# Attention without scaled probabilities: the inverse row sums go to the values' partitions and scale two heads' output at once

## The chip, the cores and the metric

The kernel runs on one core of a Trainium2 chip. The metric is the device time of one execution in microseconds (us). Three runs of the kernel before took 854.75, 860.95 and 860.27 us, median 860.27. One further execution was recorded by the profiler. The engines are TensorE (PE, with its weight loads as PEld), VectorE (DVE), ScalarE (ACT), GpSimd (POOL) and SyncE (SP, which issues nearly all transfers).

## The reference

```
scores = q @ k.T / 8                      # 4 batches, 8 heads, 576 tokens, head size 64
bias   = -(cum[q] - cum[k])               # cum = running sum of max(s, 0)
scores = where(causal, -1e9, scores + minimum(bias, 0))
attn   = exp(scores - max); attn = attn / (sum(attn) + 1e-9)
x      = attn @ v                         # heads side by side: 576 x 512 per batch
h      = relu(x @ w_in)                   # first mixer, 1024 wide
x      = (h * sigmoid(conv3(h))) @ w_out
u      = x + mix of tokens by U, V (rank 32)
out    = u + relu(u @ w_ch1) @ w_ch2      # second mixer, 2048 wide
```

All of it is float32; weights and small parameters arrive as 64-bit numbers and are decoded on the chip.

## The kernel before, in words

There are 32 heads, worked through one by one, and two heads (a *pair*) fill the 128 rows of one x tile. For a head, `scores` (L700) makes four score tiles of 128 query rows, 128 to 512 keys wide: TensorE multiplies (L690), VectorE adds the mask and takes the maximum in one pass (`top`, L651), ScalarE takes the exponential into an SBUF tile P and sums the rows on the way (`exps`, L668). The 64 query rows left over of both heads of a pair share a fifth tile (`scores4`, L730; in the profile's names `p`).

Once the fourth tile's sum is there, VectorE adds 1e-9 and inverts the four sums (L724, L725), and `normalise` (L676, L679) has GpSimd multiply P by them, row by row: four operations per head, 128 to 512 wide, and one of 576 per pair for `p`. Then `transp` (L785, L793) turns P by TensorE transposes in four groups; ScalarE (and for all but the first eight heads VectorE, which makes a low part) copies them to SBUF, and `av` (L809, L829) multiplies them with the values. The result is x transposed: its rows are the head size, two heads on top of each other, its columns are the tokens. When the second head of a pair is done, x is split into a high and a low part by ScalarE and GpSimd (L874, L875), and the first mixer (`m1_in` L893, `m1_out` L935) can use it. The mixer's matmuls for one batch run beside the next batch's attention. Behind attention come the last batch's first mixer, then the second mixer in two parts (L1174, then L1270).

P has two sets of buffers, so the exponentials of head h+2 have to wait for the transposes of head h. The q and k rows of each head are placed by SP transfers (`place`, L630) from tiles that GpSimd and VectorE split before (L618, L619).

The order of the instructions is not the order of the text. A planner (`Plan.order`, L183) lists every operation with its cost and its predecessors, and issues on each engine the earliest in the text that is ready by its own clock. Each engine, and SP's queue too, then works strictly in that order on the chip. PSUM has eight banks, given out by class (`CAPS`).

Of the kernel before, what the change touches and what calls it, by code (L numbers as in the profile page):

```python
# [8 lines left out]
F32 = mybir.dt.float32  # L9
# [35 lines left out]

RECIP = (3,)

CAPS = dict(sc=3, pt=1, av=5, h=4, y=4, tp=2, t1=4, mh=1, ma=8, my=8, mx=2)

RINGS = dict(P=2, qk=2, th=3, vv=2, qkh=1, x=2, wf=2, xs=5, g=12, hh=3, c=3, x2=4, w64=2, mh=5, o=4, snap=2, tt=4)  # L50

# [258 lines left out]
def tile_attention_moe_mixer(  # L310
# [60 lines left out]
    dram = ctx.enter_context(tc.tile_pool(name="dram", bufs=1, space=DRAM))  # L371
    r_t = dram.tile([NH, 4, 2, S], F32R, name="r_d")
    r_d = Buf(None, None, None, None, "r_d")
    u_t = [dram.tile([128, KT, S], F32, name=f"u_d{b}") for b in range(B)]
    u_d = [Buf(None, None, None, None, "u") for b in range(B)]
    ch_t = [dram.tile([128, NTOK], F32, name=f"ch_d{f}") for f in range(NF2)]
# [187 lines left out]


    xs = {}

    def p_tiles(g):
        return [ring(ap, f"P{i}_", RINGS["P"], [128, 128 * (i + 1)], F32, f"P{g}_{i}") for i in range(4)] + [
# [103 lines left out]
            186,  # L673
        )

    def normalise(t, w, r, key, keys):  # L676
        pool(
            w,
            lambda: nc.gpsimd.tensor_scalar(t[:, :w], t[:, :w], r(), 1.0, ALU.mult, ALU.mult),  # L679
            [key] + keys,  # L680
            keys,
            extra=208,
        )

    def products(h, ps, rows, q0, k0, w):
        d = st[h]

        def mms():
            for c, t in enumerate(d["qk"]):
                nc.tensor.matmul(  # L690
                    ps[:rows, :w],
                    lhsT=t[:, 0, q0 : q0 + rows],
                    rhs=t[:, 1, k0 : k0 + w],
                    start=c == 0,
                    stop=c == len(d["qk"]) - 1,
                )

        pe(16 + 1.88 * w if h in FS else 2 * mm(w, rows), mms, d["qk"], [ps])

    def scores(h, i):  # L700
        P, sm = st[h]["P"][i], st[h]["sm"]
# [14 lines left out]
        if i in RECIP:  # L716
            ns = range(max((x + 1 for x in RECIP if x < i), default=0), i + 1)
            ss = [(sm, f"s{n}") for n in ns]
            rs = [(sm, f"r{n}") for n in ns]

            def r():
                return sm[:, 8 + ns[0] : 9 + i]

            dve(2, lambda: nc.vector.tensor_scalar(r(), sm[:, 4 + ns[0] : 5 + i], 1e-9, None, ALU.add), ss, rs)  # L724
            dve(15, lambda: nc.vector.reciprocal(r(), r()), rs, rs)  # L725
            for n in ns:
                Pn = st[h]["P"][n]
                normalise(Pn, 128 * n + 128, lambda n=n: sm[:, 8 + n : 9 + n], (sm, f"r{n}"), [Pn])

    def scores4(h):  # L730

# [18 lines left out]
        for n, ps in enumerate(tiles):  # L750
            exps(
                lambda n=n: P[:, n * HS : n * HS + HS],
                ps,
                128,
                HS,
                lambda: sm[:, 1:2],
                lambda n=n: sm[:, 2 + n : 3 + n],
                (sm, "m1"),
                [(P, n), (sm, f"s{n}")],
            )  # L760
        dve(
            60,
            lambda: nc.vector.scalar_tensor_tensor(
                sm[:, 4:5], sm[:, 2:3], 1e-9, sm[:, 3:4], ALU.add, ALU.add
            ),
            [(sm, "s0"), (sm, "s1")],
            [(sm, "r")],
        )
        dve(15, lambda: nc.vector.reciprocal(sm[:, 4:5], sm[:, 4:5]), [(sm, "r")], [(sm, "r")])
        normalise(P, S, lambda: sm[:, 4:5], (sm, "r"), [(P, 0), (P, 1)])  # L770


    GROUPS = [[(0, 0, 1), (1, 1, 1)], [(0, 2, 4), (3, 3, 4)], [(1, 2, 4), (4, 4, 4)], [(2, 2, 4)]]
# [35 lines left out]
    def av(h, half):  # L809
# [53 lines left out]
        if hh % 2 == 1 and half == 1:  # L863
            th = ring(xp, "xh", RINGS["xs"], [128, S + 2], F32R, f"xh{b}_{dt}")
            tl = ring(xp, "xl", RINGS["xs"], [128, S + 2], F32R, f"xl{b}_{dt}")
            for t in (th, tl):
# [4 lines left out]
                    [],  # L871
                    [(t, "pad")],
                )
            hi_act(lambda: th[:, 1 : S + 1], x, [x], [(th, "x")], S)  # L874
            lo_pool(lambda: tl[:, 1 : S + 1], x, lambda: th[:, 1 : S + 1], [x, (th, "x")], [(tl, "x")], S)  # L875
            xs[b, dt] = (th, tl)
# [451 lines left out]
    def att_head(h):  # L1328
# [28 lines left out]
            transp(h - 1, 3)  # L1357
        if h < NH and h % 2 == 0:
            scores4(h)
        if h > 0:  # L1360
            av(h - 1, 1)

# [206 lines left out]
```

## Time and profile before

| what | value |
|---|---|
| runs | 854.75, 860.95, 860.27 us |
| profiled execution | 857.56 us, of which the span from first to last instruction 855.7 us |
| TensorE, weight loads | 95%, 86% of the span busy |
| VectorE, ScalarE, GpSimd | 71%, 54%, 43% |
| granted TensorE clock, mean | 0.995 |
| transfers | 123.31 MB, mean 144 GB/s |

The first matmul starts at 8.4 us. The share of an engine over the whole span hides the stages: attention by itself until about 100 us, attention with the first mixer until about 390, then the mixers. A wait is given to the one that came last of what an instruction waited for. A busy TensorE is not TensorE at its peak, since matmuls overlap and their ends are modelled; the weight loads' share shows more of the gaps.

### The profile page before, as it was taken

The numbers are of one execution on the slowest core, as the hardware profiler recorded it, in microseconds if no ns is written. First come the engines' busy times: TensorE is split into PE (matmuls) and PEld (weight loads), VectorE is DVE, ScalarE is ACT, GpSimd is POOL, SyncE is SP. The second block draws the span as 40 slices with busy tenths as digits, with TensorE's granted clock in tenths as the row PEclk, the third lists the DMA queues.
The fourth block names the chain that finished last, engine by engine and source line by source line (L and its number), as shares of the span: only waits on it lengthen the run. The fifth ranks groups of instructions, "written<-read, shape, count | busy, mean of one in ns | idle before, by whom it ended". The sixth has DMA issues, their size and how long they took to land. (4 is left out here: it accounts for less than half of the span.)

```text
span 855.7 us, 15636 instructions
## 1 busy us (share of the span) xinstructions
PE 813.2 (95%) x5300; PEld 738.0 (86%) x5300; DVE 610.0 (71%) x1362; ACT 459.9 (54%) x1144; POOL 365.3 (43%) x461
## 2 busy tenths in 40 slices
PE   5889899999999999999999989999999999999998
PEld 2556689889999998998999889999998888888888
DVE  6865899986997769978878998777878762323232
ACT  4776888875987668875766423223233432222211
POOL 4675777574455734457345663333344220000000
PEclk9998999999999999999999999999999999999999
DMA  6868844573455524512133336445467764545443
GB/s 198 234 161 199 202 136 121 141 188 80 122 131 146 129 58 128 149 51 82 34 115 121 118 107 204 145 144 179 138 188 235 256 203 121 163 123 165 130 123 99
DMA packets 67624, 123.31 MB, mean 144 GB/s; under 512 B 9412, under 2 KB 34884, under 8 KB 67544
## 3 DMA queue, kind: packets, MB, share of 16 engines
q1 hardware_dynamic: 67472, 122.30, 50.1%
q8 instruction: 42, 0.69, 0.3%
q14 instruction: 38, 0.31, 0.1%
q10 hardware_dynamic: 72, 0.01, 0.0%
HBM read 68.88 MB, written 28.90 MB: 114 GB/s over the span
## 5 line engine op out<-in xcount | busy, mean ns | idle before, releaser
L1270 PE MATMUL my<-mh,w 128*128 128x512 f32 (+1 forms) x560 | 158.9, 368 | 0.0
L1174 PE MATMUL ma_S<-u,W 128*128 128x288 f32 x768 | 119.2, 296 | 7.6 <-DVE s L1190 7.5
L1251 DVE SCALAR_TENSOR_TENSOR ml<-ml,mh 128x512 fp32r<-128x512 f32 (+1 forms) x80 | 51.9, 654 | 98.3 <-ACT mh L1248 98.3
L935 PE MATMUL y<-gh,w1o 128*128 128x288 f32 x512 | 118.1, 301 | 0.7 <-DVE c L914 0.4
L1270 PEld LDWEIGHTS my<-mh,w 128*128 128x128 f32 x560 | 101.6, 189 | 17.4
L1174 PEld LDWEIGHTS ma_S<-u,W 128*128 128x128 f32 x768 | 107.5, 188 | 10.2 <-DVE s L1190 10.0
L1248 ACT ACTIVATE mh<-ml 128x512 fp32r<-128x512 f32 (+1 forms) x80 | 46.9, 589 | 118.8 <-DMA ml<-ch_d 74.0
L679 POOL TENSOR_SCALAR P<-P,sm 128x128 f32<-128x128 f32 (+3 forms) x128 | 74.9, 602 | 82.2 <-DVE sm L725 61.4
L1270 PE MATMUL my<-ml,w 128*128 128x512 f32 (+1 forms) x280 | 103.0, 368 | 0.0
L1174 PE MATMUL ma_A<-u,W 128*128 128x288 f32 x576 | 92.9, 296 | 0.5 <-DVE s L1190 0.4
L935 PEld LDWEIGHTS y<-gh,w1o 128*128 128x128 f32 x512 | 86.4, 188 | 2.2 <-DVE c L914 1.1
L651 DVE CUSTOM_DVE_ANT_0 sc<-sc,mask 128x128 f32<-128x128 f32 (+2 forms) x144 | 68.8, 494 | 24.3 <-PE sc L690 17.1
L1174 PEld LDWEIGHTS ma_A<-u,W 128*128 128x128 f32 x576 | 81.8, 188 | 1.4 <-DVE s L1190 0.9
L365 POOL TENSOR_TENSOR gl<-c,gh 128x288 fp32r<-128x288 f32 x64 | 53.9, 846 | 64.3 <-ACT gh L920 60.7
L893 PE MATMUL h<-xh,w1h 128*128 128x290 f32 x256 | 80.0, 313 | 0.5 <-DVE c L914 0.5
L893 PE MATMUL h<-xl,w1h 128*128 128x290 f32 x256 | 76.4, 298 | 0.7 <-POOL xl L365 0.7
L893 PE MATMUL h<-xh,w1l 128*128 128x290 f32 x256 | 76.3, 298 | 0.0
L935 PE MATMUL y<-gl,w1o 128*128 128x288 f32 x256 | 75.1, 293 | 0.6 <-POOL gl L365 0.6
L668 ACT ACTIVATE P<-sc,sm 128x128 f32<-128x128 f32 (+3 forms) x128 | 67.5, 530 | 11.2 <-DVE sm L651 9.5
L905 DVE SCALAR_TENSOR_TENSOR c<-h,cw,c 128x288 f32<-128x288 f32 x128 | 64.3, 509 | 5.3 <-ACT c L901 4.3
L1186 ACT COPY p<-ma_A 128x288 f32<-128x288 f32 x64 | 25.5, 399 | 73.0 <-PE ma_A L1174 57.7
L362 DVE TENSOR_TENSOR tl<-pt,th 128x384 fp32r<-128x384 f32 x96 | 54.3, 566 | 12.4 <-ACT th L353 12.1
(145 smaller groups left out, 1990.6 us busy)
## 6 DMA issues: line engine op xcount, KB each, us to landing
ml<-ch_d SPq DMA_DIRECT2D x64, 256.0 KB, 2.6
ch_d<-s SPq DMA_DIRECT2D x64, 144.0 KB, 1.8
raw_w<-w_in SPq DMA_DIRECT2D x16, 512.0 KB
raw_w2a<-w_in SPq DMA_DIRECT2D x16, 512.0 KB, 4.7
raw_w2b<-w_in SPq DMA_DIRECT2D x16, 512.0 KB, 4.4
t<-qk_in SPq DMA_DIRECT2D x28, 288.0 KB, 2.9
qkA<-t SPq DMA_DIRECT2D x56, 144.0 KB, 4.0
qkA<-t SPq DMA_DIRECT2D x28, 288.0 KB, 3.0
```

Of the source, the lines that this page charges most:

```text
L362: dve(n, lambda: nc.vector.tensor_tensor(out(), src(), f32(hi()), ALU.subtract), r, w)
L365: pool(n, lambda: nc.gpsimd.tensor_tensor(out(), src(), f32(hi()), ALU.subtract), r, w, two=True)
L651: lambda: nc.vector.tensor_tensor_reduce(out=ps[:rows, :w], in0=ps[:rows, :w], in1=mask[:rows, m0 : m0 + w], scale=-0.125, scalar=3.0e38 i ...
L668: lambda: nc.scalar.activation(out(), ps[:rows, :w], ACTF.Exp, bias=low(), scale=-1.0, accum_out=total()),
L679: lambda: nc.gpsimd.tensor_scalar(t[:, :w], t[:, :w], r(), 1.0, ALU.mult, ALU.mult),
L893: nc.tensor.matmul(ps[:, :W], lhsT=ww, rhs=xx, start=kt + n == 0, stop=kt == KT - 1 and n == 2)
L905: lambda k=k: nc.vector.scalar_tensor_tensor(c(), hh[:, k : k + HS], cw[:, 3 * f + k : 3 * f + k + 1], c(), ALU.mult, ALU.add),
L935: nc.tensor.matmul(ps[:, :HS], lhsT=ww, rhs=xx(), start=f + n == 0, stop=f == NF1 - 1 and n == 2)
L1174: nc.tensor.matmul(ps[:, :HS], lhsT=ww, rhs=uu, start=k == 0, stop=k == 5)
L1248: act(n, lambda: nc.scalar.activation(mh[:, :n], raw(), ACTF.Relu), [ml], [mh])
L1251: lambda: nc.vector.scalar_tensor_tensor(ml[:, :n], raw(), 0.0, f32(mh[:, :n]), ALU.max, ALU.subtract),
L1270: nc.tensor.matmul(ys[c][dt][:, :n], lhsT=ww, rhs=xx[:, :n], start=f + k == 0, stop=f == NF2 - 1 and k == 2)
```

## The change

P stays as the exponential left it. The inverse sums of both heads of a pair go into one small tile `rr` of nine columns: four for each head and one for the shared tile. A new function `spread` transposes `rr` on TensorE to nine rows of 128 (a new PSUM class `rt`), ScalarE copies them to SBUF, SP writes them to DRAM (`rv_d`), and four more SP transfers read them back, each repeated over 64 partitions, into a tile R of 128 x 576: for each row of x the inverse sum of that token in that head. Before x is split, GpSimd multiplies x by R. The nine columns transposed hold the sums in the order of the tokens.

```diff
-    def normalise(t, w, r, key, keys):
-        pool(
-            w,
-            lambda: nc.gpsimd.tensor_scalar(t[:, :w], t[:, :w], r(), 1.0, ALU.mult, ALU.mult),
...
+    def inverse(h):
+
+        if h not in rrs:
+            rrs[h] = ring(ap, "rr", 2, [128, 9], F32, f"rr{h}")
+        return rrs[h]
...
-            for n in ns:
-                Pn = st[h]["P"][n]
-                normalise(Pn, 128 * n + 128, lambda n=n: sm[:, 8 + n : 9 + n], (sm, f"r{n}"), [Pn])
...
-        normalise(P, S, lambda: sm[:, 4:5], (sm, "r"), [(P, 0), (P, 1)])
+        dve(15, lambda: nc.vector.reciprocal(rr[:, 8:9], rr[:, 8:9]), [(rr, 8)], [(rr, 8)])
+
+    def spread(h):
+
+        rr = inverse(h)
+        ps = bank("rt", f"rt{h}")
+        pe(120, lambda: nc.tensor.transpose(ps[:9, 0:128], rr(), ident[:, 0:128]), [ident, rr], [ps])
+        rw = ring(ap, "rw", 1, [9, 128], F32, f"rw{h}")
+        act(128, lambda: nc.scalar.copy(rw(), ps[:9, 0:128]), [ps], [rw])
+        rv, d = rv_t[h // 2], Buf(None, None, None, None, f"rv{h}")
+        dma(4608, lambda: nc.sync.dma_start(out=rv, in_=rw()), [rw], [d])
+        R = ring(ap, "R", 1, [128, S], F32, f"R{h}")
+        for a in range(2):
+            half = slice(64 * a, 64 * a + 64)
+            dma(
+                131072,
+                lambda a=a, half=half: nc.sync.dma_start(
+                    out=R[half, 0:512],
+                    in_=rv[4 * a : 4 * a + 4].rearrange("a b -> (a b)").partition_broadcast(64),
+                ),
+                [d],
+                [(R, a)],
+            )
+            dma(
+                16384,
+                lambda half=half: nc.sync.dma_start(out=R[half, 512:S], in_=rv[8, half].partition_broadcast(64)),
+                [d],
+                [(R, 2 + a)],
+            )
+        return R
...
+            R = spreads.pop(h - 1)
+            pool(S, lambda: nc.gpsimd.tensor_tensor(x(), x(), R(), ALU.mult), [x, R], [x], two=True)
             hi_act(lambda: th[:, 1 : S + 1], x, [x], [(th, "x")], S)
...
+        if h < NH and h % 2 == 1:
+            spreads[h - 1] = spread(h - 1)
```

Since the planner decides, the order on every engine moves. Three places show it.

GpSimd at the third pair of the first batch, before: `P_0` to `P_3` and `p_1` are the scaling, `w1o` the low part of a weight, `t_8` the split of q and k, `xl_2` the split of the pair's x.

```order
L356 TENSOR_SCALAR t_8_738<-t_8_753 128x576
L679 TENSOR_SCALAR P_0_759<-P_0_759,sm_169 128x128
L679 TENSOR_SCALAR P_1_774<-P_1_774,sm_169 128x256
L679 TENSOR_SCALAR P_2_781<-P_2_781,sm_169 128x384
L679 TENSOR_SCALAR P_3_815<-P_3_815,sm_169 128x512
L365 TENSOR_TENSOR w1o<-wf_w_1_512_786,w1o 128x512
L679 TENSOR_SCALAR p_1_147<-p_1_147,sm_1_396 128x576
L365 TENSOR_TENSOR xl_2_117<-x_2_724,xh_2_115 128x576
L365 TENSOR_TENSOR w1o<-wf_w_2_512_847,w1o 128x512
```

The same place in the change, with the new product of x and R:

```order
L356 TENSOR_SCALAR t_8_759<-t_8_775 128x576
L365 TENSOR_TENSOR w1o<-wf_w_0_512_822,w1o 128x512
L901 TENSOR_TENSOR x_2_726<-x_2_726,R_794 128x576
L365 TENSOR_TENSOR xl_2_133<-x_2_726,xh_2_131 128x576
L365 TENSOR_TENSOR w1o<-wf_w_1_512_892,w1o 128x512
L365 TENSOR_TENSOR w1o<-wf_w_2_512_926,w1o 128x512
```

The five scalings are gone, one product stands before the split of x, and the weight parts have moved behind it.

TensorE at the first head, in the change: `pt` are its transposes of P, `tf` their copies, `sc` the third head's scores, `rt` the new transpose.

```order
L855 MATMUL av_1_294<-tf_2_296,vr_146 64x320
L683 MATMUL sc_0_313<-ws 128x128
L683 MATMUL sc_1_317<-ws 128x256
L855 MATMUL av_1_294<-tf_3_310,vr_146 64x320
L773 MATMUL rt_327<-ident,rr_220 9x128
L855 MATMUL av_1_294<-tf_1_270,vr_146 64x192
L855 MATMUL av_1_294<-tf_2_296,vr_146 64x64
L819 MATMUL pt_0_339<-ident,P_1_267 128x128 x2
```

Before, the two score tiles `sc_0` and `sc_1` stood ahead of the second group of `pt` of the first head; now they stand behind all of them, and the `rt` transpose lies between the last products with the values, with the next head's transposes behind it.

SP's queue at the second pair, in the change: `t_6` is the load of the next pair's q and k, `qkA` and `qkB` are their placement.

```order
L620 DMA t_6_469<-qk_in 128x576
L777 DMA rv_d_59<-rw_536 9x128
L783 DMA R_574<-rv_d_59 64x512
L792 DMA R_574<-rv_d_59 64x64
L783 DMA R_574<-rv_d_59 64x512
L792 DMA R_574<-rv_d_59 64x64
L640 DMA qkB_170<-r_d 4x1152
L640 DMA qkB_170<-t_6_428 64x1152
L640 DMA qkA_634<-t_6_469 64x1152
```

Here the four reads follow the write directly, and the placements of the next head stand behind; at most other pairs the loads of the next pair's q and k stand between write and reads.

## Rows read from the trace of the kernel before

**Rows 1.** The page's first part: busy us, share of the span, instructions.

```profile
PE 813.2 (95%) x5300; PEld 738.0 (86%) x5300; DVE 610.0 (71%) x1362; ACT 459.9 (54%) x1144; POOL 365.3 (43%) x461
```

**Rows 2.** Busy time by stretch: us, each engine, granted clock, DMA share, GB/s.

```profile
20.00:100.00 80.00, 69.45 (x372) 47.37 (x371) 57.20 (x153) 58.93 (x162) 53.84 (x62) 0.96 0.78 199
100.00:150.00 50.00, 47.20 (x343) 44.84 (x342) 48.22 (x131) 43.28 (x123) 38.19 (x51) 1.00 0.54 139
150.00:380.00 230.00, 225.09 (x1666) 215.35 (x1665) 186.97 (x517) 177.64 (x488) 123.48 (x200) 1.00 0.48 123
```

**Rows 3.** Waits from 20 to 100 us: total us, times, longest.

```profile
PEld pt L793 <- POOL p L679: 6.9, 5, 2.4
...
PE pt L793 <- POOL p L679: 3.4, 3, 2.0
...
PE av L829 <- DMA vr<-vP_in: 2.7, 2, 2.3
```

**Rows 4.** TensorE's waits from 100 to 380 us, the longest.

```profile
PE pt L793 <- ACT P L668: 2.0, 2, 1.0
```

**Rows 5.** Timeline around one wait: start, us, engine, what, idle before.

```profile
73.67 3.18 POOL L679 TENSOR_SCALAR P<-P,sm 128x128 f32<-128x128 f32 x4 [2.01 <-DVE sm L725]
...
74.47 0.49 ACT L668 ACTIVATE p<-sc,sm 128x288 f32<-128x288 f32 x1
...
76.81 1.69 POOL L365 TENSOR_TENSOR w1o<-wf_w,w1o 128x512 fp32r<-128x512 f32 x1
...
78.49 0.74 POOL L679 TENSOR_SCALAR p<-p,sm 128x576 f32<-128x576 f32 x1
...
79.28 0.18 PEld L793 LDWEIGHTS pt<-ident,p 128*128 128x128 f32 x1 [2.43 <-POOL p L679]
```

**Rows 6.** GpSimd's groups: busy us, mean ns, idle before them.

```profile
L679 POOL TENSOR_SCALAR P<-P,sm 128x128 f32<-128x128 f32 (+3 forms) x128 | 74.9, 602 | 82.2 <-DVE sm L725 61.4 <-ACT P L668 8.1 <-ACT raw_w2a L502 6.1
...
L365 POOL TENSOR_TENSOR xl<-x,xh 128x576 fp32r<-128x576 f32 x16 | 19.4, 1213 | 4.8 <-ACT xh L353 4.5
...
L679 POOL TENSOR_SCALAR p<-p,sm 128x576 f32<-128x576 f32 x16 | 13.3, 828 | 1.3 <-DVE sm L769 1.3
```

**Rows 7.** Busy time in three short stretches.

```profile
60.00:65.00 5.00, 3.55 (x10) 1.85 (x11) 2.08 (x3) 1.21 (x3) 3.98 (x4) 0.72 1.04 216
75.00:80.00 5.00, 3.00 (x17) 2.17 (x17) 3.56 (x12) 3.92 (x12) 5.00 (x6) 0.92 0.97 249
80.00:85.00 5.00, 5.00 (x22) 3.13 (x20) 0.35 (x2) 2.70 (x7) 3.69 (x6) 0.74 0.92 192
```

**Rows 8.** Timeline: two transposes in a row.

```profile
21.09 0.27 PE L793 MATMUL pt<-ident,P 128*128 128x128 f32 x1
...
21.20 0.27 PE L793 MATMUL pt<-ident,p 128*128 128x128 f32 x1
```

**Rows 9.** Timeline: the last pair's split and the next first-mixer matmul.

```profile
388.61 1.28 POOL L365 TENSOR_TENSOR xl<-x,xh 128x576 fp32r<-128x576 f32 x1 [2.42 <-ACT xh L353]
...
390.54 0.30 PE L893 MATMUL h<-xh,w1h 128*128 128x290 f32 x1
```

**Rows 10.** Transfers: issues, KB each, us to landing; and one issue's time on SP.

```profile
ch_d<-s SPq DMA_DIRECT2D x64, 144.0 KB, 1.8
...
qkB<-t SPq DMA_DIRECT2D x28, 288.0 KB, 3.7
...
59.64 1.11 SPq L638 DMA_DIRECT2D qkA<-t  x1
```

**Rows 11.** Timeline: a decode step beside GpSimd's scaling, and one alone.

```profile
74.95 0.77 DVE L515 SCALAR_TENSOR_TENSOR wf_w<-raw_w,wf_w 128x512 int32<-128x512 int32 x1
...
85.62 0.69 DVE L515 SCALAR_TENSOR_TENSOR wf_w<-raw_w,wf_w 128x512 int32<-128x512 int32 x1
```

**Rows 12.** Timeline of ScalarE: a pair's last exponential, its last copy of x.

```profile
81.13 0.69 ACT L668 ACTIVATE P<-sc,sm 128x512 f32<-128x512 f32 x1
...
95.56 0.42 ACT L851 COPY x<-av 64x320 f32<-64x320 f32 x1 [0.19 <-PE av L829]
```

More of the change, by code (lines that the diff above doesn't have):

```diff
@@ L46 @@
 RECIP = (3,)
-CAPS = dict(sc=3, pt=1, av=5, h=4, y=4, tp=2, t1=4, mh=1, ma=8, my=8, mx=2)
+CAPS = dict(sc=3, pt=1, av=5, h=4, y=4, tp=2, t1=4, mh=1, ma=8, my=8, mx=2, rt=1)
 RINGS = dict(P=2, qk=2, th=3, vv=2, qkh=1, x=2, wf=2, xs=5, g=12, hh=3, c=3, x2=4, w64=2, mh=5, o=4, snap=2, tt=4)
@@ L373, in tile_attention_moe_mixer @@
     r_d = Buf(None, None, None, None, "r_d")
+    rv_t = [dram.tile([9, 128], F32, name=f"rv_d{h}") for h in range(NH // 2)]
     u_t = [dram.tile([128, KT, S], F32, name=f"u_d{b}") for b in range(B)]
@@ L566, in tile_attention_moe_mixer @@
     xs = {}
+    rrs, spreads = {}, {}
     def p_tiles(g):
@@ L674, in exps @@
         )
-    def normalise(t, w, r, key, keys):
-        pool(
-            w,
-            lambda: nc.gpsimd.tensor_scalar(t[:, :w], t[:, :w], r(), 1.0, ALU.mult, ALU.mult),
[L680 to L683, printed above, removed]
     def products(h, ps, rows, q0, k0, w):
@@ L718, in scores @@
             ss = [(sm, f"s{n}") for n in ns]
-            rs = [(sm, f"r{n}") for n in ns]
+            rr = inverse(h - h % 2)
+            c = 4 * (h % 2)
             def r():
-                return sm[:, 8 + ns[0] : 9 + i]
-            dve(2, lambda: nc.vector.tensor_scalar(r(), sm[:, 4 + ns[0] : 5 + i], 1e-9, None, ALU.add), ss, rs)
-            dve(15, lambda: nc.vector.reciprocal(r(), r()), rs, rs)
-            for n in ns:
-                Pn = st[h]["P"][n]
-                normalise(Pn, 128 * n + 128, lambda n=n: sm[:, 8 + n : 9 + n], (sm, f"r{n}"), [Pn])
+                return rr[:, c + ns[0] : c + i + 1]
+            dve(2, lambda: nc.vector.tensor_scalar(r(), sm[:, 4 + ns[0] : 5 + i], 1e-9, None, ALU.add), ss, [(rr, c)])
+            dve(15, lambda: nc.vector.reciprocal(r(), r()), [(rr, c)], [(rr, c)])
     def scores4(h):
@@ L763, in scores4 @@
             lambda: nc.vector.scalar_tensor_tensor(
-                sm[:, 4:5], sm[:, 2:3], 1e-9, sm[:, 3:4], ALU.add, ALU.add
+                rr[:, 8:9], sm[:, 2:3], 1e-9, sm[:, 3:4], ALU.add, ALU.add
             ),
             [(sm, "s0"), (sm, "s1")],
-            [(sm, "r")],
+            [(rr, 8)],
         )
-        dve(15, lambda: nc.vector.reciprocal(sm[:, 4:5], sm[:, 4:5]), [(sm, "r")], [(sm, "r")])
-        normalise(P, S, lambda: sm[:, 4:5], (sm, "r"), [(P, 0), (P, 1)])
+        dve(15, lambda: nc.vector.reciprocal(rr[:, 8:9], rr[:, 8:9]), [(rr, 8)], [(rr, 8)])
+    def spread(h):
+        rr = inverse(h)
+        ps = bank("rt", f"rt{h}")
[23 more added lines that the diff above has]
+        return R
     GROUPS = [[(0, 0, 1), (1, 1, 1)], [(0, 2, 4), (3, 3, 4)], [(1, 2, 4), (4, 4, 4)], [(2, 2, 4)]]
```

## The prediction

> **What bounds the kernel now.** First the page's shares of busy time [rows 1]: TensorE is busy 95% of the span, so what can be won is its idle time, and what is added to it costs. Then the table by stretch [rows 2], because one share over the whole hides where that idle time lies. From 20 to 100 us, the stage with attention and little else, TensorE is busy 69.45 of 80 us and its weight loads only 47.37, while no other engine exceeds 58.93: nobody is full, so this stage is bound by chains of waits. From 150 to 380 us TensorE is busy 225.09 of 230 us: the first mixer's matmuls fill what attention leaves. Between them, from 100 to 150 us, VectorE is busy 48.22 of 50 us and is the bound.
>
> Then who is waited for. From 20 to 100 us the longest wait of TensorE's weight loads is for GpSimd's scaling of the tile that a pair's two heads share (`p`): 6.9 us in 5 waits; the matmuls behind show 3.4 us of the same waits, which I don't add [rows 3]. From 100 to 380 us the longest wait that TensorE's view names is 2.0 us, for ScalarE's exponentials; GpSimd's scaling isn't there [rows 4]. So the scaling costs time in the first 100 us and is covered later.
>
> One such wait in order of time [rows 5]: GpSimd scales four P tiles from 73.67 for 3.18 us, then works on a weight (76.81), and reaches `p` at 78.49. `p`'s last exponential had ended at 74.96. TensorE's weight load got its turn at 79.28, after 2.43 us idle. The reader should see that the wait is not the scaling's 0.74 us but the queue on GpSimd ahead of it.
>
> **The change part by part.**
>
> *Scaling P goes.* 128 operations of 602 ns on P and 16 of 828 ns on `p`, 74.9 + 13.3 = 88.2 us of GpSimd [rows 6]. Nothing of it is on TensorE itself; what counts is who waited. Removed at most: the 6.9 us [rows 3]. What is late next is the exponential; in the example it was done 4.3 us before TensorE got to go (79.28 − 74.96), so I take all of it: **−6.9**, with bounds of −6.9 and −3.4 (if only the waits that the matmuls show are won).
>
> *The clock.* TensorE's granted clock was 0.92 from 75 to 80 us and 0.74 from 80 to 85 [rows 7], which means part of the time at 1.2 instead of 2.4 GHz: 0.08·5 + 0.26·5 = 1.7 us of work at full speed lost. Just before, TensorE had idled in the wait shown above, 2.0 us in the matmuls' own count [rows 3]. Without that wait I take it back: **−1.7** (bounds −1.7 and 0). The other dip, 60 to 65 us (0.72), followed a wait of up to 2.3 us for the values' transfer [rows 3], which the change doesn't touch: 0.
>
> *P buffers come free earlier in the first 100 us.* There are two sets of P, so the exponentials of head h+2 wait for the transposes of head h. Beyond the 6.9, TensorE idles 80 − 69.45 − 6.9 = 3.7 us there. I take about half, **−2** (bounds 0 and −3.7).
>
> *Behind 100 us.* TensorE idles 2.8 + 4.9 us in 100 to 380 [rows 2], over many short waits. VectorE is full up to 150, and the change takes no instruction from it. I take **−1.5** (bounds 0 and −4.9, all that idles behind 150).
>
> *The 16 transposes of the inverse sums* are added to TensorE. Back-to-back transposes start 0.11 us apart [rows 8]; TensorE has no cover from 100 us on: 16 × 0.11 = **+1.8**. The trace of before doesn't show one with a 9-column source: bounds 0, if each falls into a wait, and 4.3, if each costs the full 0.27 us of a row.
>
> *The order, and waits on TensorE.* The transpose stands in TensorE's queue between products with V, and behind it lie the rest of that head and the next head's transposes. If the reciprocals are late, all of these wait. But the same head's P transposes need the same exponentials, so it is rarely the latest: 0; upper bound 2.0, as much again as TensorE waits for exponentials from 100 to 380 us [rows 4].
>
> *Copies on ScalarE*, 16 of 9 x 128: hidden, ScalarE is busy 177.64 of 230 us behind 150. If the cover went (20 to 100 us, 58.93 of 80), about 0.4 us each in a chain that has slack; 0.
>
> *GpSimd's new product, x times R,* 16 of 128x576 with two inputs: the row of the same shape is 1,213 ns, 19.4 us in all [rows 6], in place of 88.2. It lies ahead of the split of x. For most pairs the next mixer matmuls are far away. Only the last pair has none behind it: its split ended at 388.61 + 1.28 = 389.89, and the next first-mixer matmul in TensorE's queue stands at 390.54 [rows 9], 0.65 us of slack against 1.21: **+0.6** (bounds 0 and 3.0, if R is late too).
>
> *80 transfers.* One write and four broadcast reads per pair, 288 KB into SBUF each time, 4.7 MB against 123 MB. Where the transfers are already full, 60 to 65 us with a DMA share of 1.04 at 216 GB/s [rows 7], 288 KB take 1.4 us; of the four pairs before 100 us I let one fall there and one half: **+1** (bounds 0 and 5.5, all four). On SP, an issue takes up to 1.11 us in a row [rows 10], and the reads wait for the write to land: 1.8 us for the nearest row, `ch_d` written to DRAM.
>
> Sum against the profiled execution's own 857.56 us (span 855.7): −6.9 − 1.7 − 2 − 1.5 + 1.8 + 0.6 + 1 = −8.7, so **849 us**. The profiled execution lies 2.7 us under the median of the runs shown, 860.27, and inside their spread. About 1% is what a measurement of this kernel can tell from no change; the forecast is 1.0% under the profiled execution and 1.3% under the median, so it stands near that bound and is counted 7 in 10 as over it.
>
> **The rivals.**
>
> *A. The waits only change their name (22%).* TensorE gets to `p` earlier, and then waits for ScalarE's exponentials, for the copies behind the transposes, or for transfers, which already are 2.7 us of it [rows 3]; VectorE's full stretch from 100 to 150 us swallows what was won before it. For: no engine but VectorE is near full there, and TensorE's waits are short and of many sources. Against: in the example, `p` was ready 4.3 us early. Price: of the gain the 3.4 us of the matmuls' own waits remain, with +1.8 − 1.7 + 0.6 + 1: 857.6 − 1.7 ≈ **856**, within 1%.
>
> *B. The whole stage runs freer (12%).* Head after head is a loop through P's two sets, and four microseconds out of its chain pay in every round; GpSimd quiet also lets VectorE go faster. For: weight loads idle 32.6 of 80 us, far more than the matmuls' rows admit. Beside GpSimd's scaling a decode step of VectorE took 0.77 us, alone 0.69 [rows 11]; the 16 weight blocks of the first mixer have three decode steps each, and 48 × 0.08 is 3.8 us in the stretch that VectorE bounds or just before it. Against: the transfers, 78% busy from 20 to 100 us, leave at most 18 us, and get more to do. Price: −8.7 − 3.8 and about 4 more of the chains: **841**. The Trainium skill has a rule for this (GPSIMD Engine Reference, section 8, Key points): GpSimd shares its SBUF interfaces with VectorE and contends with those VectorE instructions that run in a two-port mode or have two SBUF inputs. The rows agree, by 0.08 us an instruction. By the rows the sum would be 3.8 us lower; by the rule, which gives no figure, the 19.4 us of new products would contend as well and take some of that back.
>
> *C. A queue is held up (16%), the other side.* SP issues in order. Write, landing, and four reads form a chain that other transfers stand behind: in SP's new order the reads of the second pair follow the write at once, and the next heads' q and k stand behind. For each pair SP stands still about 1.8 us for the landing and up to 4 × 1.11 us for the issues. GpSimd, too, works in order: if R isn't there, the product holds up the splits of q, k, values and gate behind it. It decides against the change when R lands later than the pair's x is whole. At the fourth pair that distance was 81.13 + 0.69 to 95.56 + 0.42 [rows 12]: 14 us. R's way is the reciprocal and the transpose (under 1 us of work), the copy, 1.8 for the landing, up to 4.4 for the issues and 3.7 for a read like `qkB` [rows 10]: about 11 us with no queueing at all; two waits of 2 us in queues use up the rest. Price: if half of an issue chain of 1.8 + 1.1 comes onto TensorE's path for 12 of 16 pairs, +17, less the gain: 857.6 + 17 − 8.7 ≈ **866**. Against: after 100 us the transfers are half idle (share 0.48 to 0.54), and GpSimd has 70 us more room.
>
> **How the numbers follow.** The forecast's case has 50% and reaches from 843 to 855 us by the bounds above; A has 22%, B 12%, C 16%. The range that leaves out 2 in 10, the deeper half of B and the upper part of C: **840 to 863**. Faster by over 1%: 0.7 × 50% + B's 12% = 47%; within 1%: 15% + 22% = 37%; slower: 16%.
>
> **What would show it.** In the changed kernel's waits from 20 to 100 us the line of TensorE waiting for GpSimd's scaling is gone, and no line of 5 us or more for the exponentials, for `rr` or for R stands in its place. TensorE's idle time there falls from 10.6 to about 3 us and the granted clock of 75 to 85 us is full. GpSimd is busy about 70 us less. The last pair's split ends some 8 us earlier than at 389.89 us, and all behind that stays as long as it was. I am wrong if TensorE's idle time stays at 10 us under other names (A), if the last head moves forward by 15 us (B), or if SP or GpSimd show waits for R's transfers with q, k or gate operations behind them that TensorE then waits for (C).

## The result and the profile after

The change is slower: 866.77 us as the median of five runs (865.97 to 870.66) against 857.52 for the kernel before in runs of the same round (854.75 to 860.95), a ratio of 1.011 with a 95% interval of [1.0087, 1.0133]. That is 9 us more, small but clear of the scatter; a time of 849 us, some 9 less, had been forecast. The profiled execution took 866.77 us, its span 865.0 us.

The page's first part after the change, with busy us, share and instructions of each engine, answers to [rows 1]:

```profile
PE 822.6 (95%) x5316; PEld 746.7 (86%) x5316; DVE 610.2 (71%) x1362; ACT 464.4 (54%) x1160; POOL 305.2 (35%) x333
```

GpSimd has 60 us less to do (305.2 for 365.3) and nothing came of it. TensorE is busy longer than its 16 added transposes explain. The table by stretch (us, busy time of each engine, granted clock, DMA share, GB/s) answers to [rows 2]; below it are three of the short stretches, the first two answering to [rows 7]:

```profile
20.00:100.00 80.00, 69.44 (x370) 46.51 (x368) 52.37 (x151) 57.79 (x161) 31.84 (x28) 0.96 0.81 207
100.00:150.00 50.00, 44.32 (x298) 41.85 (x299) 47.54 (x115) 41.61 (x115) 30.29 (x33) 0.93 0.55 146
150.00:380.00 230.00, 227.37 (x1691) 218.48 (x1690) 190.02 (x533) 179.84 (x504) 90.36 (x120) 1.00 0.54 137
...
75.00:80.00 5.00, 1.64 (x11) 1.26 (x11) 4.97 (x10) 4.51 (x12) 2.87 (x3) 1.00 1.04 205
80.00:85.00 5.00, 4.15 (x12) 1.85 (x13) 1.16 (x3) 1.74 (x5) 3.46 (x3) 0.67 1.03 204
100.00:105.00 5.00, 4.14 (x22) 4.05 (x22) 4.33 (x10) 3.90 (x12) 4.39 (x6) 0.71 0.98 217
```

From 20 to 100 us TensorE idles 10.56 us, before 10.55: not a tenth was won. From 100 to 150 us it idles 5.7 us where it idled 2.8, and 45 matmuls fewer fall into that stretch. The clock is below the full level of 2.4 GHz for part of the time from 80 to 85 us (0.67) and from 100 to 105 us (0.71), each time behind an idle TensorE. The waits from 20 to 100 us (total us, times, longest) answer to [rows 3]:

```profile
PE av L855 <- DMA vr<-vP_in: 4.2, 1, 4.2
...
PEld pt L819 <- ACT P L670: 3.2, 7, 1.0
...
PE sc L683 <- ACT x L877: 2.3, 1, 2.3
```

No wait for GpSimd's scaling is left. In its place stand one wait of 4.2 us for the values' transfer (it was 2.3 at most), one of 2.3 for ScalarE's copy of x, and the exponentials. GpSimd's groups (busy us, mean ns), ScalarE's copies and the transposes, which answer to [rows 6] and [rows 8], and two of SP's waits:

```profile
L901 POOL TENSOR_TENSOR x<-x,R 128x576 f32<-128x576 f32 x16 | 24.2, 1516 | 8.5 <-ACT x L877 5.4 <-DVE x L883 3.0
L365 POOL TENSOR_TENSOR xl<-x,xh 128x576 fp32r<-128x576 f32 x16 | 20.4, 1280 | 9.8 <-ACT xh L353 9.7
...
L773 PE MATMUL rt<-ident,rr 128*9 128x128 f32 x16 | 4.6, 289 | 0.5 <-DVE rr L725 0.5
L775 ACT COPY rw<-rt 9x128 f32<-9x128 f32 x16 | 4.0, 251 | 1.3 <-PE rt L773 1.2
...
SPq L783 <- DMA rv_d<-rw: 18.6, 10, 4.2
SPq L777 <- ACT rw L775: 13.1, 8, 6.0
```

A product takes 1.52 us, not the 1.21 of the split of the same shape. TensorE hardly waits for the inverse sums (0.5 us in all). SP does wait for the chain of R: 18.6 us for the write to land and 13.1 us for ScalarE's copy ahead of it, 31.7 us in total. Whether anybody waits for SP in turn is what the experiments had to tell. The last pair, in order of time (start, us), answers to [rows 9]:

```profile
391.32 1.67 POOL L901 TENSOR_TENSOR x<-x,R 128x576 f32<-128x576 f32 x1 [1.61 <-DVE x L883]
393.78 1.35 POOL L365 TENSOR_TENSOR xl<-x,xh 128x576 fp32r<-128x576 f32 x1 [0.79 <-ACT xh L353]
...
395.43 0.30 PE L921 MATMUL h<-xh,w1h 128*128 128x290 f32 x1
```

Its split ends at 395.13 us, 5.2 us later than before (389.89), where 8 us earlier had been expected. So 5 us of the 9 are lost by the end of attention and the rest behind it, where nothing of the change runs.

### The profile page after: what moved, and what is told of

It reads as the page before. It is cut to its first block, busy times and chain, and to the rows that moved or that the text cites. A ratio compares the mean times of both kernels' runs of the same rounds, so it can differ in the third digit from the quotient of the medians.

```text
span 865.0 us, 15612 instructions
## 1 busy us (share of the span) xinstructions
PE 822.6 (95%) x5316; PEld 746.7 (86%) x5316; DVE 610.2 (71%) x1362; ACT 464.4 (54%) x1160; POOL 305.2 (35%) x333
## 5 line engine op out<-in xcount | busy, mean ns | idle before, releaser
L1202 PE MATMUL ma_A<-u,W 128*128 128x288 f32 x576 | 95.0, 301 | 2.6 <-DVE s L1218 2.6
L1202 PEld LDWEIGHTS ma_A<-u,W 128*128 128x128 f32 x576 | 83.8, 192 | 3.5 <-DVE s L1218 3.3
L921 PE MATMUL h<-xh,w1h 128*128 128x290 f32 x256 | 82.2, 321 | 2.7 <-DVE c L942 2.4
L365 POOL TENSOR_TENSOR gl<-c,gh 128x288 fp32r<-128x288 f32 x64 | 56.5, 891 | 64.3 <-ACT gh L948 55.5
L683 PE MATMUL sc<-qkB 128*128 128x128 f32 (+3 forms) x168 | 55.5, 344 | 5.8 <-ACT x L877 2.3
L819 PE MATMUL pt<-ident,P 128*128 128x128 f32 x320 | 60.7, 277 | 0.0
```

The lines of the kernel that those rows point to most:

```text
L365: pool(n, lambda: nc.gpsimd.tensor_tensor(out(), src(), f32(hi()), ALU.subtract), r, w, two=True)
L683: nc.tensor.matmul(ps[:rows, :w], lhsT=t[:, 0, q0 : q0 + rows], rhs=t[:, 1, k0 : k0 + w], start=c == 0, stop=c == len(d["qk"]) - 1,)
L819: nc.tensor.transpose(pt[:, o + rows - 128 : o + rows], d["P"][i][:, 128 * j : 128 * j + 128], turn)
L921: nc.tensor.matmul(ps[:, :W], lhsT=ww, rhs=xx, start=kt + n == 0, stop=kt == KT - 1 and n == 2)
L1202: nc.tensor.matmul(ps[:, :HS], lhsT=ww, rhs=uu, start=k == 0, stop=k == 5)
```

## The experiments

Two explanations stood against each other: the added parts cost far more than they were priced at (a held queue, as in rival C), or the gain of the removal is lost by the order that the planner makes anew. The planner lists all operations with planned costs and orders each engine's queue anew whenever an operation is taken out, added or given another cost. An operation can also be *planned but not issued*: the order is then that of the kernel with it, and only its work is gone.

**The parts of the change, one at a time (four kernels).** First neither P nor x is scaled and nothing takes the scalings' place; the planner orders anew:

```diff
-            spreads[h - 1] = spread(h - 1)
+            pass
...
-            pool(S, lambda: nc.gpsimd.tensor_tensor(x(), x(), R(), ALU.mult), [x, R], [x], two=True)
```

> Neither P nor x is scaled: the changed kernel without the inverse sums' way to x (no transpose, copy, transfers, product; the output is not divided by the sums), ordered anew by the planner. Theory Q (the transfers of R hold up SP, the weights of the first mixer come late, VectorE's work moves into its full stretch): about 850 us, 7 below before. Theory O (the new order itself costs, whatever is in it): 862 or more. Theory K (the clock: each stretch at half clock behind an idle TensorE costs 1.7 us, and the changed kernel has seven entries of them against two): the time follows the number of such stretches, two or three of them give 850 to 853, six or more give 860.

Measured: 858.28 us, ratio to before (858.53 in this round) 0.9989 [0.9964, 1.0014]. Without any scaling, and without anything added, the kernel is as slow as before. Theory Q's 850 fails here; theory O has the direction, but not its 862. Second, the order of the kernel before on every engine, with the 144 scalings planned but not issued:

```diff
-            lambda: nc.gpsimd.tensor_scalar(t[:, :w], t[:, :w], r(), 1.0, ALU.mult, ALU.mult),
+            lambda: None,
```

> The kernel before in its own order on every engine, with the 144 scalings of GpSimd not issued (the output is not divided by the sums). It prices the waits for the scaling alone: by the prediction's first term 6.9 us less than before, about 850 us; by rival A (the waits change their name) 855 or more. Theories Q and O both say 850; K says that it stays at 855 or more if the half-clock stretches increase.

Measured: 851.84 us, 0.9932 [0.9909, 0.9956]: 6.7 us faster by the medians, 5.8 by the ratio. These two kernels issue the same work, and the order alone makes 6.4 us between their medians; their intervals don't touch. Theory K can't explain it: leaving out the one at the very end, both profiled executions have three stretches at half clock. Third, the order of the change with the whole chain of R (transposes, copies, transfers, products) planned but not issued:

```diff
-        pe(120, lambda: nc.tensor.transpose(ps[:9, 0:128], rr(), ident[:, 0:128]), [ident, rr], [ps])
+        pe(120, lambda: None, [ident, rr], [ps])
...
-            pool(S, lambda: nc.gpsimd.tensor_tensor(x(), x(), R(), ALU.mult), [x, R], [x], two=True)
+            pool(S, lambda: None, [x, R], [x], two=True)
```

> The order of the changed kernel on every engine, with the transposes of the inverse sums, their copies, transfers and products not issued (the output is not divided by the sums). Theory Q: 850 to 853 us, since nothing holds up SP. Theory O: 864 or more, since the order stayed. Theory K: 857 plus or minus 1.7 for each half-clock stretch more or less than four.

Measured: 859.64 us, 1.0018 [0.9998, 1.0038]. The change's own order, with nothing of the chain in it, is 7.8 us slower than the old order with nothing of the scaling in it. That again refutes Q (850 to 853), and O's 864 isn't reached. Fourth, the same order with the transposes, copies and products, but R's transfers for the first pair only (the others multiply by that R):

```diff
-        dma(4608, lambda: nc.sync.dma_start(out=rv, in_=rw()), [rw], [d])
+        dma(4608, lambda: (nc.sync.dma_start(out=rv, in_=rw()) if h == 0 else None), [rw], [d])
```

> The changed kernel in its own order with the transfers of R issued for the first pair alone; the transposes, copies and products stay, and all products use the first pair's R (the output is scaled by wrong sums). Theory Q: 852 to 855 us, the products and transposes cost little. If the product on GpSimd or the transposes on TensorE cost the time: 863 or more. Theory O: 864 or more.

Measured: 864.34 us, 1.0077 [1.0046, 1.0108]. So the transposes, copies and products cost 4.7 us in this order. By the medians the transfers add 2.4 us; but the intervals of the two ratios overlap, and the profiled executions (867.23 without, 866.77 with them) show no difference, so their share isn't settled.

How an order loses time can be read on SP. The issues in order of time (start, us) in the second kernel, which has the order of before:

```profile
68.52 0.48 SPq L638 DMA_DIRECT2D qkB<-t  x1
69.64 1.10 SPq L638 DMA_DIRECT2D qkA<-t  x2
70.83 0.99 SPq L591 DMA_DIRECT2D vr<-vP_in  x1
71.87 0.73 SPq L638 DMA_DIRECT2D qkA<-t  x1
72.71 1.35 SPq L525 DMA_DIRECT2D raw_w<-w_in  x2
```

and in the third, with the order of the change and no R anywhere, with TensorE's longest wait from 20 to 100 us under it:

```profile
70.93 1.11 SPq L640 DMA_DIRECT2D qkA<-t  x2
72.55 0.34 SPq L526 DMA_DIRECT2D raw_w<-w_in  x1
73.19 0.46 SPq L640 DMA_DIRECT2D qkA<-t  x1
74.02 0.34 SPq L593 DMA_DIRECT2D vr<-vP_in  x1
...
PE av L852 <- DMA vr<-vP_in: 4.9, 3, 3.7
```

In the old order both blocks of weights (512 KB each) stand behind the values' transfer, and the values go out at 70.8 us. In the new one a block stands ahead, they go out at 74.0, and TensorE waits 3.7 us for them. That is the wait of 4.2 us in the change, and R's transfers are not needed for it, since here there are none. Head 8 then starts at 85.8 us instead of 77.8. Starts of the first matmuls of a kind (of the scores for heads 8 and 12), in us, read off the five traces, one execution each:

| kernel | head 8 | head 12 | first mixer's output | second mixer | its second part | span |
|---|---|---|---|---|---|---|
| before | 84.5 | 136.1 | 131.9 | 458.6 | 654.8 | 855.7 |
| old order, no scaling | 77.8 | 134.4 | 130.3 | 456.0 | 651.3 | 852.2 |
| new order, no R | 85.8 | 141.7 | 134.6 | 457.8 | 657.5 | 858.5 |
| new order, no transfers | 88.0 | 144.3 | 137.5 | 463.7 | 663.2 | 865.4 |
| after | 86.2 | 142.8 | 136.0 | 462.7 | 663.6 | 865.0 |

Between the second and third line the second mixer's first part takes 195.3 and 199.7 us, though neither kernel has any work there that the other lacks. So the late values are not where the order's loss ends up: of the 8.0 us at head 8 only 1.8 are left where the second mixer starts, and 4.4 of the 6.3 us between the two spans arise in its first part. There the granted clock is 1.00 in the old order (456 to 652 us) and 0.98 in the new one (457 to 658 us).

**Three tries at the cause in the order.** VectorE has its full stretch when weights are decoded, and the new order decodes the eighth block of weights at 62.7 us, before at 51.5. So one theory was that the weights' place decides. The whole change, with the planner shown the scalings as ghosts (planned, never issued):

```diff
+                pool(128 * n + 128, lambda: None, [(rr, c), Pn], [Pn], extra=208)
```

> The changed kernel, complete, but the planner still counts GpSimd's 144 scalings as work of their old length and place; nothing is issued for them. The planner so thinks a head as long as before, and orders anew around that. Theory W (told that a head is shorter, the planner lets attention run ahead of the first mixer's weights, whose decoding then falls into VectorE's full stretch): the weights come as early as before, and the time is e2's 851.8 plus about 5 for transposes, copies and products and 2 for transfers, 859. Rival (any new order costs some 6 us, by chance): 864 or more.

Measured: 869.96 us, 1.0146 [1.0115, 1.0177]. The whole change, and the kernel with no scaling at all, each with the weights one head earlier:

```diff
-W1_AT = [0, 1, 1, 2, 3, 4, 5, 5, 6, 7, 7, 8, 9, 10, 10, 11]
+W1_AT = [0, 0, 0, 1, 2, 3, 4, 4, 5, 6, 6, 7, 8, 9, 9, 10]
```

> The changed kernel, complete, with the first mixer's weights asked for one head earlier. Theory W: the 16 weights are decoded before the full stretch again and some 5 us come back, 861 or 862. Rival (the weights' lateness is a sign, not the cause): 866 as the changed kernel, or slower, since the loads now meet the transfers of q and k.

Measured: 866.67 us, 1.013 [1.0081, 1.018].

> As e1 (no scaling of P or of x, ordered anew; the output is not divided by the sums), with the first mixer's weights asked for one head earlier. Theory W: back to e2's 852. Rival: 858 as e1.

Measured: 857.44 us, 0.999 [0.9972, 1.0009]. The theory of the weights falls: in these kernels the eighth block is decoded at 49.0, 53.8 and 52.9 us, about as early as before, and none is faster by more than the scatter.

**The change in the old order.** The scalings planned but not issued, and the chain of R hung onto operations that are there anyway: the transpose of the sums behind the first group of P's transposes, the reads at the third group, the product right ahead of ScalarE's copy of x. For pairs whose copy of x is put off, the product reads a later pair's R.

```diff
+            if h % 2 and g == 0:
+                spread_row(h, pt)
+            if h % 2 and g == 2:
+                spread_in(h)
...
+                    nc.gpsimd.tensor_tensor(x(), x(), R(), ALU.mult),
                     nc.scalar.copy(th[:, 1 : S + 1], x()),
```

> The whole change carried out in the order of the kernel before: every other instruction stands where it stood on its engine, the scalings of P are gone, and transposes, copies, transfers and products of R are put in beside the same heads' work. The output is complete. Theory O (the new order is the largest part of the loss): e2's 851.8 plus 1.8 for the transposes, 2.4 for the transfers and 1 to 2 for products, 857, so no slower than before. Rival (what was added costs by itself what the changed kernel lost): 863 or more.

Measured: 879.74 us, 1.0268 [1.0233, 1.0304]. The waits of ScalarE from 20 to 400 us, and of SP, in this kernel (total us, times, longest):

```profile
ACT xh L911 <- POOL x L910: 20.5, 12, 2.6
...
SPq L451 <- ACT rw L450: 57.6, 15, 13.0
...
SPq L457 <- DMA rv_d<-rw: 10.3, 11, 1.9
```

ScalarE stands 20.5 us behind GpSimd's products, and SP up to 13.0 us behind one copy. Without a plan of its own the chain holds up queues, as rival C had it, and 28 us are lost against the same order without it. The time is the one that the text above gives to its rival, but these waits come from where the chain was hung, so the run doesn't tell what the added parts must cost in the old order. In the order planned with it, the whole change is 15 us above that kernel (866.77 − 851.84), 13 us less than with the chain hung in, its new order included.

**Is the old order a lucky one?** The kernel before with all its work, the planner told that a scaling takes 48 ns less, then 52 more (by the traces, where tiles of one name are not told apart, at least some 300 of TensorE's 5,300 matmuls move in each; the 700 in the text below counts a moved row twice, where it stood and where it stands):

```diff
-            extra=208,
+            extra=160,
```

> The kernel before with all its work, the planner only told that a scaling takes 48 ns less than it had been told (160 for 208): every instruction stays, some 700 of 4039 TensorE rows stand elsewhere. Theory N (the order that the kernel before has is better than its neighbours, and a new order costs some 6 us whatever it is for): 862 to 866. Rival M (orders planned anew scatter about the one of before by 1 or 2 us, so the loss in the order of the change is its own): 855.5 to 859.5.

Measured: 861.21 us, 1.0054 [1.0032, 1.0077].

```diff
-            extra=208,
+            extra=260,
```

> As the kernel with the shorter planned scaling, in the other direction (260 for 208). Theory N: 862 to 866. Rival M: 855.5 to 859.5.

Measured: 854.54 us, 0.9972 [0.9952, 0.9992]. The change itself, with a longer planned product, and with its chain written later:

```diff
-            pool(S, lambda: nc.gpsimd.tensor_tensor(x(), x(), R(), ALU.mult), [x, R], [x], two=True)
+            pool(S, lambda: nc.gpsimd.tensor_tensor(x(), x(), R(), ALU.mult), [x, R], [x], extra=1300)
```

> The whole change, the planner told that a product of x with R takes 1.82 us, as the trace after shows it beside other work (1.86), where it counted 1.36. Theory N (most orders cost what this one costs): 864 to 869. Rival M' (the order of the change is a bad draw, made with a product that the plan has too short): 856 to 862.

Measured: 865.25 us, 1.0105 [1.0072, 1.0138].

```diff
-        if h < NH and h % 2 == 1:
-            spreads[h - 1] = spread(h - 1)
         if h > 0:
             av(h - 1, 1)
+        if h < NH and h % 2 == 1:
+            spreads[h - 1] = spread(h - 1)
```

> The whole change, with the transposing of the inverse sums, their copy and their transfers written behind the last product of values of the head instead of ahead of it, so that the plan puts them later. Theory N: 864 to 869. Rival M' (another place of the chain leaves the stages ahead of it as they were): 856 to 862. If the transfers then come too late for the product, the longest wait for R goes above 3 us and the time above 870.

Measured: 861.46 us, 1.0051 [1.0026, 1.0076]. Neither theory holds as written. One and the same work of the kernel before takes 854.5, 858.0 and 861.2 us by its order alone, so an order is worth 3 to 4 us in either direction. The change in its orders takes 861.5 to 870.0. The better order of the change shows the other side of the wait above; its row of the stretch, and SP's issues:

```profile
20.00:100.00 80.00, 70.73 (x381) 47.16 (x379) 59.56 (x158) 60.36 (x169) 36.78 (x33) 0.97 0.77 210
...
69.03 0.34 SPq L593 DMA_DIRECT2D vr<-vP_in  x1
69.84 0.33 SPq L526 DMA_DIRECT2D raw_w<-w_in  x1
```

The values go out at 69.0 us, ahead of the weights, TensorE doesn't wait for them, and 11 more matmuls fit into the same 80 us than in the change.

**The border into the second mixer: six misses.** In the names of the trace `ma` are the second mixer's first products, and `mh` those that end the last batch's mix of tokens and stand among them. From the first `ma` matmul to the next `mh` matmul take 13.8 to 13.9 us in all seven orders planned without the chain, and 16.2 to 17.9 in all seven planned with it, the one that issues nothing of it included (16.3). TensorE waits there for VectorE's first addition, behind decodings of weights. Four kernels put the decoding of the second pair of weight blocks earlier in the plan:

```diff
+    plan.bias = -1
     for _ in load_w2a(1, u1p):
         pass
     bring_w2a(2)
+    plan.bias = 0
```

> The whole change, with the second pair of blocks of the second mixer's weights planned ahead of the work of its stage. In the trace after (and in all seven kernels planned with the new chain) VectorE's last decoding of that pair ends 4.3 us behind the first ma matmul, ahead of the first addition that empties ma_S, and TensorE waits 2.4 us for that addition at 467.55, 3.3 us in all until ma_A goes on; in the kernels planned without the chain it ends 1.9 us behind, and that wait is not there. From ma to my the change takes 200.9 us and before 196.2. Theory T (4 to 5 of the 9 us are lost at that border, by the order of VectorE alone): 861.5 to 864, ma to my 196 to 198, the wait at ma_A gone. Rival U (the work of VectorE has only been moved ahead, and the first mixer ends later by as much): 865 to 869, ma later by 3 to 5 us.

Measured: 870.01 us, 1.0145 [1.0113, 1.0177].

> The chain written later (861.46 measured) and the decoding planned earlier, together. Theory T: the two add, 856 to 859, no slower than the kernel before. Rival U: 860 to 864.

Measured: 865.46 us, 1.0082 [1.0055, 1.0109].

> The kernel before with the same earlier decoding, as the control: its order has the decoding out of the way already. Theory T: 856 to 860, no change from its 858. If it gains 3 us or more, the border costs the kernel before too, and what the change lost there is not its own.

Measured: 864.9 us, 1.0081 [1.0052, 1.0111].

> The chain written later, the decoding earlier, and the planned length of the product at 1.82 us: one more order of the same work. Theory T: 856 to 860. A spread of more than 4 us against the kernel without the longer product says that single orders differ by more than any of the single steps.

Measured: 868.28 us, 1.0128 [1.0095, 1.016]. The three that have a counterpart without the edit lost 3.2, 4.0 and 6.2 us against it: the first `ma` block itself came some 50 us earlier, into the first mixer (at 406.0 instead of 458.6 us in the kernel before). The last two put two decodings behind the addition and left TensorE's order as it was:

```diff
+            late = sorted((o for o in self.decode if at[o] < at[self.empty]), key=lambda o: at[o])[-2:]
+            for o in ops[at[late[0]] : at[self.empty]]:
+                if o not in late and o.preds & set(late):
+                    late.append(o)
+            ops = [o for o in ops if o not in late]
+            i = ops.index(self.empty) + 1
+            ops[i:i] = late
```

> The whole change in its own order, TensorE's order the same row for row; of VectorE's order at the border into the second mixer only the last two decodings of weights, and the four or so instructions of other engines that need them, stand behind the first addition that empties ma_S instead of ahead of it. From the first ma to the first mh the change takes 17.8 us and the kernel before 13.8. Theory T (the border costs 4 us, of the change's 9): 862 to 864, first ma to first mh 14 to 15 us, the wait of 2.4 us at ma_A gone. Rival U (the decoding is needed at once, and its next reader waits instead): 865.5 to 868, first ma to first mh 16 us or more, or the same loss behind it.

Measured: 880.03 us, 1.0263 [1.0228, 1.0298].

> The chain written later (861.46 us measured; 16.3 us from the first ma to the first mh), with the same two decodings behind that addition. Theory T: 858.5 to 860, level with the kernel before. Rival U: 861 to 864.

Measured: 875.04 us, 1.0208 [1.0177, 1.0239]. TensorE's longest waits from 440 to 560 us in the first of the two:

```profile
PE t L1011 <- ACT xth L365: 11.4, 1, 11.4
PE ma_S L1217 <- DVE s L1233: 4.4, 2, 2.3
PE t L1011 <- DVE xtl L374: 3.7, 1, 3.7
```

These six were aimed wrongly. The trace names all these tiles `wf_w2a`, and the decodings that stand right ahead of the addition are those of the third pair; the edit moved the second pair's, the last of which starts 49 us ahead of the first `ma` matmul. Their readers on ScalarE moved with them, and TensorE waits 11.4 us for that queue. So what makes the border 2.4 to 4.1 us longer was not tried, and stays open.

No order of the change was found that beats the kernel before. The fastest kernel with all its work is the one before in the order with the longer planned scaling, 854.54 us.

## Why the prediction was wrong, step by step

- **Scaling P goes, −6.9: not refuted, but not measured apart.** The old order without the scalings gains 6.7 us by the medians. That is the size of this term, but the sum had 12.1 for the removal, with the clock's −1.7, the P buffers' −2 and −1.5 behind 100 us on top. Those 5.2 us were not there even with the old order. In the two profiled executions head 8 starts 6.7 us earlier, and the second mixer only 2.6.
- **The step that failed: the order.** The prediction counted what the planner moved as 0 ("it is rarely the latest: 0") and carried the waits of the old order over into the new one. Taking the scalings out and planning anew gives the gain back: +6.4 without the chain (858.28 − 851.84), +7.8 with it in the plan and nothing issued (859.64 − 851.84). The runs show one place in the first 100 us, the weights ahead of the values on SP, whose delay is mostly made up later. They show that the border of the second mixer is longer by the order too, not which row does it. Which part of the order costs how much stays open. The shares close: −6.7 + 7.8 + 7.1 (the next point) is 8.2, and the other 1.0 us is the difference of the kernel before in the two rounds, 858.53 and 857.52.
- **The added parts, +3.4: too small.** From the new order with nothing issued to the whole change are 7.1 us: 4.7 for transposes, copies and products where 1.8 and 0.6 stood, and 2.4 by the medians for transfers where 1 stood, not settled. The product's price came from the split, 1.21 us; it takes 1.52, 24.2 us in all for 19.4. And it slows VectorE, which no term had. The decoding of the first mixer's weights (busy us, mean ns) in the new order with no R and, under it, with the products and no transfers:

```profile
L516 DVE SCALAR_TENSOR_TENSOR wf_w<-raw_w,wf_w 128x512 int32<-128x512 int32 x32 | 24.7, 777 | 0.2
L506 DVE TENSOR_SCALAR wf_w<-raw_w 128x512 int32<-128x512 int32 x16 | 8.2, 513 | 7.7 <-ACT raw_w L503 7.6
```

```profile
L516 DVE SCALAR_TENSOR_TENSOR wf_w<-raw_w,wf_w 128x512 int32<-128x512 int32 x32 | 26.4, 831 | 0.2
L506 DVE TENSOR_SCALAR wf_w<-raw_w 128x512 int32<-128x512 int32 x16 | 9.4, 589 | 7.2 <-ACT raw_w L503 7.0
```

  The same 48 instructions take 2.9 us longer in the same order, in or near the stretch that VectorE bounds; in the change itself, with means of 804 and 589 ns, 2.0 us. Four of the 48 overlap a product. Two of these make 1.8 of the 2.9 us: an L516 took 1.43 us where it took 0.68 without products, an L506 1.50 where it took 0.41, and in the change both take as long. How the 4.7 us divide between this, the transposes and the copies was not measured apart. The Trainium skill says that GpSimd contends with VectorE for SBUF where VectorE's instruction has two inputs or runs in a two-port mode (GPSIMD Engine Reference, section 8, Key points). The step at L516 has two inputs and agrees. The one at L506 has one, and no run here shows whether it runs in such a mode.
- **The clock, −1.7: it came out the other way.** The old order without the scalings has the wait gone and its mean granted clock is 0.994, beside 0.993 for the kernel before; that of the change is 0.982. More on this stands below.
- **The range was narrower than its terms.** The forecast's case was said to reach from 843 to 855 us by the bounds. Added up, the bounds give 840 and 869, and the measured time lies inside.
- **Rival A was the mechanism in the first 100 us.** The waits changed their name, 10.55 us of idle time to 10.56. Its price of 856 was too low: it let the old order's other waits stand and counted 1.7 us won by the clock.
- **Rival B fell.** VectorE's decoding did get faster than before, from 849 to 804 ns and from 663 to 589, 2.6 us of the 3.8 it counted. The last head starts at 371.6 us and not at 352; before it was 367.2.
- **Rival C gave the number, 866, and not the cause.** SP does wait 31.7 us for R's chain. Without these transfers the time is still 864.3 us, so the held queue explains 2.4 of the 9 us by the medians, and the number was met by luck. Where the chain is unplanned, C is real, and costs more than its price.
- **The signs it named.** The scaling's wait is gone, as forecast; a wait of over 4 us stands in its place; the clock from 80 to 85 us is 0.67 and not full; GpSimd is busy 60 us less (70 forecast); the last split is 5.2 us later.

**The clock goes with the order.** The granted clock of nearly every execution is on record: 0.980 to 0.986 in the five of the change (mean 0.982), 0.985 to 1.000 in 77 of the kernel before (mean 0.993). One minus the clock, times the span, is work at full speed lost: 15.6 us against 6.1 on the mean. The 9.5 us between them are as much as the whole loss. The mean clock is 0.990 to 0.994 in all seven kernels planned without the chain (0.985 where it was then hung in), and 0.979 to 0.989 in all twelve planned with it. This doesn't show that the clock is the cause: no run changed it alone. Nor does a lost microsecond go with a whole one of time: among the 77 executions of the kernel before, 1 us more of lost work goes with 0.5 us more of time. And it isn't all: between the two kernels that were compared first, with neither scaling nor chain, the lost work differs by 1.7 us (7.0 in the new order, 5.3 in the old) and the time by 6.4.

Two rows of the second mixer before, then the same place after, 4 us later, with TensorE's waits there from 458 to 655 us (total us, times, longest):

```profile
460.00:480.00 20.00, 20.00 (x149) 19.28 (x148) 14.94 (x30) 11.48 (x23) 8.09 (x9) 1.00 0.52 177
500.00:520.00 20.00, 19.58 (x147) 19.34 (x146) 17.53 (x36) 6.95 (x15) 12.05 (x11) 1.00 0.51 170
```

```profile
460.00:480.00 20.00, 17.81 (x120) 16.63 (x120) 14.67 (x21) 11.04 (x21) 8.06 (x6) 0.91 0.45 141
500.00:520.00 20.00, 17.70 (x113) 17.36 (x114) 17.05 (x35) 5.33 (x11) 12.38 (x11) 0.83 0.31 104
...
PE ma_S L1202 <- DVE s L1218: 6.4, 8, 2.0
PE ma_A L1202 <- DVE s L1218: 2.6, 2, 2.2
```

A clock of 0.91 and 0.83 over 20 us means 1.8 and 3.4 us of work at full speed lost, by the same reckoning as in the prediction; waits of 2.2 and 2.0 us for VectorE stand right ahead of these dips.

## What to carry to other kernels

Where a planner sets the order, taking work out changes the order of all the rest: price the removal at the old order and the new order apart, by planning the removed work and not issuing it. Give the planner's constants a small nudge before believing any gain of under 1%; here it moved one and the same work by 3 to 4 us either way. A chain of small steps through four queues that is not in the plan costs through what stands behind it in each queue, 28 us here. Look for what now stands ahead of the next transfer that somebody needs, not only for waits on the chain itself, and compare the granted clock over all executions of both kernels.

## What was not expected of the hardware

An idle TensorE is not always followed by a lower clock. The kernel before idles 4.9 of 20 us and keeps its full level, and the change with the later chain idles 4.7 in the same place and does not. In both, two waits make most of it, of 2.0 and 2.4 us in the first and 2.0 and 2.2 in the second. The rows are one of each, in that order:

```profile
480.00:500.00 20.00, 15.09 (x108) 14.15 (x107) 20.00 (x32) 6.99 (x13) 14.93 (x11) 1.00 0.27 92
```

```profile
480.00:500.00 20.00, 15.29 (x101) 14.22 (x100) 20.00 (x31) 6.59 (x12) 15.74 (x12) 0.88 0.25 85
```

And GpSimd's product of two tiles in SBUF takes 1.52 us where its difference of the same shape takes 1.28, beside the same engines; why was not tried.
